# First batch of a block-sorted attention with a gated MLP: V blocks by transposes, K copied in output order

## The chip, the cores and the metric

One Trainium2 chip, one of its cores. The metric is the device time of one execution in microseconds (us), and the time of a kernel is the median of its runs. A profile is one execution taken by the hardware profiler; it names the engines PE (TensorE matmul), PEld (TensorE weight load), DVE (VectorE), ACT (ScalarE), POOL (GpSimd) and SP (the queue of SyncE, from which some DMAs are issued).

## The reference, cut to what matters

```python
B, H, S, D = 4, 8, 768, 64;  n_blocks = 8;  block = 96
P = sort_net                                   # [B, H, 8, 8]
for _ in range(5):                             # exp, then rows and columns normalised
    P = exp(P - max);  P = P / (rowsum + 1e-9);  P = P / (colsum + 1e-9)
k_sorted = einsum('bhij,bhjcd->bhicd', P, k_blocks)     # blocks of K and V are mixed by P
v_sorted = einsum('bhij,bhjcd->bhicd', P, v_blocks)
scores = q_blocks @ k_sorted^T / sqrt(D)                # within each block of 96 rows
x = softmax(scores) @ v_sorted                          # -> [B, S, H*D]
h = relu(x @ w_in);  u, v = halves of h                 # w_in [512, 1024]
v_n = layer-normalised v
v_s = w_spatial @ v_n + b_spatial                       # w_spatial [768, 768]
out = (u * v_s) @ w_out                                 # w_out [512, 512]
```

## The kernel before, in words

The four batches go through two stages. Attention of batch b makes x; the MLP (class `Gmlp`) of batch b is interleaved with the attention of batch b + 1, step by step, in an order written out by hand. Attention of batch 0 has no MLP beside it: it is a stretch of its own at the start of the kernel. PE, DVE, ACT and POOL each run their instructions in the order of the program; only the DMAs of SP are free of that order.

**Loads.** `load_heads` (L88) brings q, k or v of one batch from DRAM and casts it to bf16: 768 KB each in SBUF. All these loads are issued from POOL, one behind the other, in the order q0, v0, k0, w_in (1,024 KB), v1, w_spatial (1,152 KB), q1, k1, w_out (512 KB). The row p of such a tile holds the six sequence rows 6p to 6p+5 (index g), so a block of 96 rows takes 16 partitions.

**P.** `sinkhorn` (L149) normalises P on DVE and ACT. `spread` (L173) turns all 4 x 8 matrices with eight small matmuls, copies the result, spreads it over the partitions with one more matmul and copies it to `prep_sb`. `make_pdiag` (L191) multiplies it with a mask: `pdiag[b]` holds, for each head, a 128 x 128 matrix that mixes the eight blocks. For batch 0 this is four products on DVE of two heads each; for batches 1 to 3 it is one product of eight heads each on POOL, which are issued at the same point of the program. POOL then makes `b_bc`, a reordered copy of b_spatial.

**Attention.** Heads go in pairs (hp 0 to 3).

- `vmix` mixes V of a pair on PE (two matmuls of 384 columns) and copies the result to `vm`. After each second pair, SP writes half of `vm` to DRAM (`vd`, L245) and reads it back as `vb` (L246), with the 96 rows of a block on 96 partitions.
- `qtr` (L251) transposes q of two pairs.
- `ktr` (L266) mixes and transposes K of a pair in one go: twelve matmuls with K as the weights and `pdiag` as the data, into a PSUM tile with columns (g, it). One copy of 768 elements per partition (L277) reorders it to (it, g), the order of the sequence. The copy's loops run in the order of its source: PSUM is read in one run, and SBUF is written in steps of six elements (12 bytes).
- `score` n takes half the blocks of a pair: eight matmuls and an exp on ACT. `attend` n multiplies with `vb` on PE (eight matmuls), and DVE divides by the row sums (a reciprocal and a product).
- `xtr` transposes x of two pairs; the MLP needs all of it.

PSUM has four buffers, which all steps take in turn (`ps_tile`, L77). `warm` issues matmuls whose results nobody reads.

**The order for batch 0** (L438 to 455): sinkhorn, qtr 0 and 1, six warm matmuls, `spread`, the products of batch 0 on DVE and of the others on POOL, all four vmix, then ktr, score and attend, and xtr 0 and 1. For each later batch the steps stand in the list at L460; there `load` fetches q, k and v of batch b + 2, once the `vb` of batch b + 1 has arrived.

Of the kernel before, what the change touches and what calls it, by code (L numbers as in the profile page):

```python
# [9 lines left out]
BF16 = mybir.dt.bfloat16  # L10
# [19 lines left out]
def kernel(  # L30
# [27 lines left out]
    VW = D + 1  # L58
# [14 lines left out]
    small = ctx.enter_context(tc.tile_pool(name="small", bufs=4))  # L73
# [3 lines left out]
    def ps_tile(dt=FP32):  # L77
        return psum.tile([128, 2, 512 if dt == FP32 else 1024], dt, name="ps", tag="ps")
# [6 lines left out]
    b_nat = pers.tile([128, S], FP32)  # L85
    nc.sync.dma_start(out=b_nat, in_=_raw_ap(moe_b_spatial, 0, [[0, 128], [1, S]]))

    def load_heads(x, b, name):  # L88
        t = ld.tile([128, H, G * D], BF16, name=name, tag=name)
        nc.gpsimd.dma_start(  # L90
            out=t,
            in_=_raw_ap(x, b * H * S * D, [[G * D, 128], [S * D, H], [1, G * D]]),
        )
        return t

    v_in, k_in, q_in = {}, {}, {}

    ident_bf = const.tile([128, 128], BF16)
    make_identity(nc, ident_bf)
    a16 = const.tile([16, 128], BF16)  # L100
# [2 lines left out]
        out=a16.rearrange("p (j t) -> p j t", t=TB),  # L103
        in_=a16.rearrange("p (j t) -> p j t", t=TB),
# [3 lines left out]
    sel16 = const.tile([8, 128], BF16)  # L108
# [17 lines left out]
    q_in[0] = load_heads(q, 0, "q_in")  # L126
    v_in[0] = load_heads(v, 0, "v_in")
    k_in[0] = load_heads(k, 0, "k_in")
    w_in_sb = pers.tile([128, KC, DFF], BF16)
    nc.gpsimd.dma_start(out=w_in_sb, in_=moe_w_in.rearrange("(kc p) f -> p kc f", p=128))  # L130
    v_in[1] = load_heads(v, 1, "v_in")
    wsp_nat = pers.tile([128, G, S], BF16)
    nc.gpsimd.dma_start(out=wsp_nat, in_=moe_w_spatial.rearrange("(p g) s -> p g s", g=G))
    q_in[1] = load_heads(q, 1, "q_in")
    k_in[1] = load_heads(k, 1, "k_in")
# [35 lines left out]
    prep_sb = pers.tile([128, NB * BH], BF16)  # L171

    def spread():  # L173
        pt_ps = ps_tile()
        for i in range(NB):
            nc.tensor.matmul(
                pt_ps[0:NB, 0, i * BH:(i + 1) * BH],
                lhsT=p_bf[:, i, :], rhs=ident_bf[0:BH, 0:BH],
                start=True, stop=True,
            )  # L180
        pt_sb = pers.tile([NB, NB * BH], BF16)
        nc.vector.tensor_copy(out=pt_sb, in_=pt_ps[0:NB, 0, 0:NB * BH])
        warm(2)
        prep_ps = ps_tile()
        nc.tensor.matmul(prep_ps[:, 0, 0:NB * BH], lhsT=sel16, rhs=pt_sb, start=True, stop=True)
        nc.vector.tensor_copy(out=prep_sb, in_=prep_ps[:, 0, 0:NB * BH])
        warm(4)

    pdiag = [pd_pool.tile([128, H, NB, TB], BF16, name="pdiag") for _ in range(B)]

    def make_pdiag(b, eng, h0, n):  # L191
        eng.tensor_mul(  # L192
            out=pdiag[b][:, h0:h0 + n],
            in0=_raw_ap(mask16, 0, [mask16.ap[0], [0, n], [TB, NB], [1, TB]]),
            in1=_raw_ap(prep_sb, b * H + h0, [prep_sb.ap[0], [1, n], [BH, NB], [0, TB]]),
        )

    b_bc = pers.tile([128, S], FP32)
# [21 lines left out]
    class Attention:  # L220
        def __init__(self, b):
            self.b = b
            self.pd = pdiag[b].rearrange("p h i t -> p h (i t)")
            self.vm = vm_tiles[b % 2]
            self.q, self.k, self.e = {}, {}, {}

        def vmix(self, hp, eng):
            t = ps_tile()
# [34 lines left out]
                self.q[hp] = qT[:, x, :].rearrange("p (g i t) -> p i g t", g=G, i=NB)  # L263
            copy(eng, qT, t[:, :, 0:S])

        def ktr(self, hp, eng):  # L266
            t = ps_tile().rearrange("p x c -> p (x c)")
            for g in range(G):
                for hh in range(2):
                    nc.tensor.matmul(  # L270
                        t[hh * 64:hh * 64 + 64, g * 128:(g + 1) * 128],
                        lhsT=k_in[self.b][:, 2 * hp + hh, g * D:(g + 1) * D],
                        rhs=self.pd[:, 2 * hp + hh, :],
                        start=True, stop=True,
                    )
            kT = qk_pool.tile([128, S], BF16, name="kT", tag="k")
            copy(  # L277
                eng,
                kT.rearrange("p (it g) -> p g it", g=G),
                t[:, 0:S].rearrange("p (g it) -> p g it", g=G),  # L280
            )
            self.k[hp] = kT

        def score(self, n):
            hp, ih = n // 2, n % 2
# [150 lines left out]
    with tc.manual_schedule(engines={ET.PE, ET.DVE, ET.Activation, ET.Pool}):  # L436
        a = Attention(0)
        sinkhorn()  # L438
        warm(4)
        a.qtr(0, ACT), a.qtr(1, ACT)  # L440
        warm(6)
        spread()
        for h in range(0, H, 2):
            make_pdiag(0, DVE, h, 2)
        for b in range(1, B):
            make_pdiag(b, nc.gpsimd, 0, H)
        nc.gpsimd.tensor_copy(
            out=b_bc.rearrange("p (g c) -> p g c", g=G),
            in_=b_nat.rearrange("p (c g) -> p g c", g=G),
        )  # L450
        a.vmix(0, ACT), a.vmix(1, DVE), a.vmix(2, ACT), a.vmix(3, DVE)
        a.ktr(0, ACT), a.ktr(1, DVE), a.score(0), a.score(1), a.ktr(2, DVE), a.ktr(3, DVE)
        a.score(2), a.score(3), a.score(4), a.attend(0), a.score(5), a.attend(1)
        a.attend(2), a.score(6), a.attend(3), a.score(7), a.attend(4), a.attend(5)
        a.xtr(0, ACT), a.attend(6), a.attend(7), a.xtr(1, ACT)
        for b in range(B):
            m = Gmlp(b)
            last = b == B - 1
            a = None if last else Attention(b + 1)
            steps = """  # L460
                vproj0 vmix0 vproj1 vmix1 vmix2 vproj2 vmix3 qtr0 norm wsp0 uproj0 ktr0 ktr1 wsp1
                uproj1 qtr1 score0 score1 wsp2 uproj2 ktr2 ktr3 wsp3 load uproj3 score2 score3
                wsp4 wsp5 spatial0 attend0 attend1 score4 score5 spatial1 attend2
                attend3 spatial2 score6 score7 attend4 attend5 spatial3 attend6 attend7 xtr0
                oproj0 oproj1 xtr1 oproj2
            """.split()
            for step in steps:
                name, n = step.rstrip("0123456789"), int(step[-1]) if step[-1].isdigit() else None
                if name == "wsp":
                    if b == 0:  # L470
                        wsp_unit(n)
                elif name == "load":
                    if b + 2 < B:
                        gate = small.tile([1, 2], BF16, name="gate", tag="gate")
                        nc.gpsimd.tensor_copy(out=gate[:, 0:1], in_=a.vb[0:1, 0, 1, 0, 0:1])  # L475
                        v_in[b + 2] = load_heads(v, b + 2, "v_in")
                        q_in[b + 2] = load_heads(q, b + 2, "q_in")
                        k_in[b + 2] = load_heads(k, b + 2, "k_in")
                elif name in ("vproj", "uproj"):
                    getattr(m, name)(n)  # L480
                elif name == "spatial":
                    m.spatial(n, DVE if last and n == FC - 1 else nc.gpsimd)
                elif name == "norm":
                    m.norm()
                elif name == "oproj":
                    m.oproj(n, ACT)
                elif not last:
                    if name in ("vmix", "ktr"):
                        getattr(a, name)(n, ACT if n % 2 == 0 else DVE)
                    elif name in ("qtr", "xtr"):  # L490
                        getattr(a, name)(n, DVE)
                    else:
                        getattr(a, name)(n)
# [30 lines left out]
```

## Time and profile before

| | us |
|---|---|
| median of 3 runs | 217.22 (214.38 to 217.23) |
| profiled execution, its own time | 216.15 |
| its span, from the first to the last instruction | 214.4 |
| PE busy in the span | 167.0 (78%) |
| DVE busy | 128.6 (60%) |
| ACT busy | 94.1 (44%) |
| POOL busy | 47.7 (22%) |
| mean clock granted to TensorE | 0.884 of full speed |

Starts are counted from the first instruction. The 1.75 us between the execution's time and its span lie around the span. [...] Busy shares are averages over stretches with different limits, so the views below go by stretch.

### The profile page before, as it was taken

Reading aid. Unit: us, or ns where it says so; the run is one execution under the profiler, and the core shown is the slowest. Engines: PE = TensorE matmul, PEld = TensorE weight load, DVE = VectorE, ACT = ScalarE, POOL = GpSimd, SP = SyncE. Lnnn points to the kernel's source line nnn. Section 1 sums busy time; section 2 is a strip of 40 time slices with the busy share of each in tenths; the row PEclk is TensorE's granted clock in tenths of the full one; section 3 lists DMA queues with packets and bytes.
Section 4 is the critical chain, followed back from the end, with each engine's and each line's share of the span. In section 5 each row is a group of like instructions: output and inputs, shape, how many; then the busy total and the mean of one; then the engine's idle time right before and its main releaser. Section 6 shows DMA issues by size and latency. Waiting matters only on the chain.

```text
span 214.4 us, 3826 instructions
## 1 busy us (share of the span) xinstructions
PE 167.0 (78%) x1621; PEld 102.0 (48%) x1630; DVE 128.6 (60%) x229; ACT 94.1 (44%) x105; POOL 47.7 (22%) x46
## 2 busy tenths in 40 slices
PE   3293550189894988999986889999868898999981
PEld 0250250177353556665454566555535665556530
DVE  4719974066179856782598548717965586185430
ACT  3151570053457484105666842148649321446031
POOL 8809500000000313350000535300000363000710
PEclk9999555555599799999998799999979999999998
DMA  5999999980006399404236798052550000510015
GB/s 99 201 204 211 221 238 235 213 152 0 0 3 213 85 169 202 76 0 196 102 133 168 103 204 136 0 199 98 173 130 0 3 0 2 234 63 0 0 71 222
DMA packets 23041, 25.50 MB, mean 119 GB/s; under 512 B 753, under 2 KB 19697, under 8 KB 22897
## 3 DMA queue, kind: packets, MB, share of 16 engines
q0 software_dynamic: 13680, 12.19, 35.9%
q1 hardware_dynamic: 9344, 13.08, 18.7%
q8 instruction: 12, 0.20, 0.4%
q14 instruction: 5, 0.03, 0.1%
HBM read 27.98 MB, written 9.49 MB: 175 GB/s over the span
## 4 chain that ended last, share of the span: by engine, by line
PE 49%; DVE 22%; DMA 14%; ACT 9%; POOL 3%; issue 2%; DVEq 0%; ACTq 0%; SPq 0%; POOLq 0%
PE ps L402 13%; PE ps L355 9%; PE ps L423 8%; PE ps L387 7%; DMA vb<-vd 6%; DMA vd<-vm 4%; DVE vs L408 4%; DVE kT L215 4%; ACT kT L213 4%; DMA q_in<-in_q_dram 4%; DVE pdiag L192 3%; DVE vm L215 3%; PE ps L313 3%; POOL gt L412 2%; DVE stats L366 2%; PE ps L335 2%
## 5 line engine op out<-in xcount | busy, mean ns | idle before, releaser
L412 POOL TENSOR_TENSOR gt<-vs,u_sb 128x768 bf16<-128x768 f32 x15 | 24.6, 1640 | 79.0 <-DVE rec L321 57.0
L298 ACT ACTIVATE ex<-ps 96x768 bf16<-96x768 f32 x32 | 24.3, 804 | 33.5 <-PE ps L291 22.3
L402 PE MATMUL ps<-wspT,v_sb 128*128 128x384 bf16 x192 | 33.3, 326 | 1.7 <-ACT ex L298 1.4
L387 PE MATMUL ps<-xt,w_in_sb 128*128 128x384 bf16 x128 | 26.4, 359 | 4.9 <-DVE kT L215 2.7
L215 DVE CAST kT<-ps 128x768 bf16<-128x768 f32 x9 | 24.3, 2726 | 9.4 <-PE ps L270 9.4
L366 DVE BATCH_NORM_STATS2 stats<-v_sb 128x6 f32<-128x512 bf16 x24 | 16.2, 676 | 18.5 <-ACT v_sb L363 18.4
L213 ACT COPY o_sb<-ps 128x1024 f32<-128x1024 f32 x12 | 12.1, 1012 | 33.4 <-PE ps L423 33.4
L408 DVE TENSOR_TENSOR vs<-ps,b_bc 128x768 f32<-128x768 f32 x16 | 15.3, 958 | 18.2 <-PE ps L402 18.0
L313 PE MATMUL ps<-vb,ex 96*96 96x65 bf16 x256 | 17.1, 225 | 10.5 <-DMA vb<-vd 10.0
L355 PE MATMUL ps<-w_in_sb,xt 128*128 128x512 bf16 x92 | 24.2, 405 | 1.3 <-ACT xt L213 1.1
L402 PEld LDWEIGHTS <-v_sb 128*128 128x128 bf16 x192 | 18.3, 98 | 12.9 <-issue 1.6
L423 PE MATMUL ps<-w_out_sb,gt 128*128 128x512 bf16 x92 | 22.5, 379 | 1.9 <-POOL gt L412 1.0
L322 DVE TENSOR_TENSOR x_sb<-ps,rec 96x512 bf16<-96x512 f32 x32 | 22.0, 687 | 1.1
L313 PEld LDWEIGHTS <-ex 96*96 96x96 bf16 x256 | 16.1, 142 | 12.3 <-DMA vb<-vd 10.3
L213 ACT CAST kT<-ps 128x768 bf16<-128x768 f32 x7 | 19.1, 2728 | 2.3 <-PE ps L270 2.3
L387 PEld LDWEIGHTS <-w_in_sb 128*128 128x128 bf16 x128 | 12.8, 104 | 14.4 <-issue 8.0
L393 ACT ACTIVATE u_sb<-ps 128x768 bf16<-128x768 f32 x16 | 13.6, 873 | 9.6 <-PE ps L387 9.6
L291 PE MATMUL ps<-qT,kT 64*96 64x96 bf16 x256 | 12.1, 228 | 7.3 <-ACT kT L213 5.0
L363 ACT ACTIVATE v_sb<-ps 128x1024 bf16<-128x1024 f32 x12 | 12.3, 1023 | 10.1 <-PE ps L355 10.1
L355 PEld LDWEIGHTS <-xt 128*128 128x128 bf16 x96 | 9.8, 104 | 13.0 <-issue 2.1
L475 POOL COPY gate<-vb 1x1 bf16<-1x1 bf16 x2 | 0.4, 178 | 69.6 <-DMA vb<-vd 69.6
L423 PEld LDWEIGHTS <-gt 128*128 128x128 bf16 x96 | 8.6, 98 | 12.8 <-POOL gt L412 3.1
(66 smaller groups left out, 179.0 us busy)
## 6 DMA issues: line engine op xcount, KB each, us to landing
out_dram<-o_sb SPq DMA_DIRECT2D x12, 512.0 KB, 2.8
vd<-vm SPq DMA_DIRECT2D x8, 390.0 KB, 2.8
vb<-vd SPq DMA_DIRECT2D x8, 390.0 KB, 4.2
q_in<-in_q_dram POOLq DMA_DIRECT2D x4, 768.0 KB, 10.6
v_in<-in_v_dram POOLq DMA_DIRECT2D x4, 768.0 KB, 8.9
k_in<-in_k_dram POOLq DMA_DIRECT2D x4, 768.0 KB, 13.6
wsp_nat<-in_moe_w_spatial_dram POOLq DMA_DIRECT2D x1, 1152.0 KB, 25.9
w_in_sb<-in_moe_w_in_dram POOLq DMA_DIRECT2D x1, 1024.0 KB, 17.3
```

The costliest lines, as they stand in the source:

```text
L213: nc.scalar.copy(out=out, in_=in_)
L215: nc.vector.tensor_copy(out=out, in_=in_)
L298: nc.scalar.activation(out=e.rearrange("p h i c -> p h (i c)"), in_=t[0:BLK, :, 0:NB // 2 * BLK], func=AF.Exp, scale=scale,)
L313: nc.tensor.matmul(t[0:BLK, hh, ii * VW:(ii + 1) * VW], lhsT=self.e[n][:, hh, ii, :], rhs=self.vb[:, i, h // (H // 2), h % (H // 2), :], s ...
L322: nc.vector.tensor_mul(out=self.x[:, ih * (NB // 2):(ih + 1) * (NB // 2), hp * 128:hp * 128 + 128] .rearrange("p i (h d) -> p h i d", h=2) ...
L355: nc.tensor.matmul(t[:, x, :], lhsT=self.xt[kc][:, g * 128:(g + 1) * 128], rhs=w_in_sb[:, kc, DH:DFF], start=(kc == 0), stop=(kc == KC - 1),)
L366: nc.vector.bn_stats(out=stats, in_=v_sb[:, x, :])
L387: nc.tensor.matmul(t[:, x, 0:HW], lhsT=w_in_sb[:, kc, mc * 128:(mc + 1) * 128], rhs=self.xt[kc][:, x * HW:(x + 1) * HW], start=(kc == 0), ...
L402: nc.tensor.matmul(t[:, x, 0:HW], lhsT=self.v[g][:, mc * 128:(mc + 1) * 128], rhs=wspT[:, g, x * HW:(x + 1) * HW], start=(g == 0), stop=(g ...
L408: nc.vector.tensor_add(out=vs, in0=t[:, :, 0:HW], in1=b_bc.rearrange("p (x c) -> p x c", x=2),)
L412: eng.tensor_mul(out=gt.rearrange("p (x c) -> p x c", x=2), in0=vs, in1=self.u[mc].rearrange("p (x c) -> p x c", x=2),)
L423: nc.tensor.matmul(t[:, x, :], lhsT=self.gt[mc][:, g * 128:(g + 1) * 128], rhs=w_out_sb[:, mc, :], start=(mc == 0), stop=(mc == FC - 1),)
```

## The change

- Loads are issued in the order q0, k0 (both ahead of the constants that POOL builds), v0, w_in, w_spatial, v1, k1, q1, w_out.
- `spread(b, nb)` handles nb batches from b on. Batch 0 goes first, alone; batches 1 to 3, with their products on POOL and the copy `b_bc`, follow at the step `spread` in the middle of the attention of batch 0. The products of batch 0 on DVE are two: heads 0 and 1, and heads 2 to 7. Ten of the twelve warm matmuls around `spread` are dropped.
- `mixed_t` is the old `ktr`, now for K or V. Its copy names the loops in the order of its output: SBUF is written in one run, and PSUM is read in steps of 128 elements (512 bytes). All batches use it for K.
- In batch 0, V takes the way of K: `vtr` mixes and transposes it, and `vblk` transposes each block back (eight transposes of 128 x 96 and one copy of 96 x 1,024 into `vb`). `vmix` with its two DMAs per half is not used in batch 0; the later batches keep it.
- The attention of batch 0 has a new order, given as a string; A and D name the engine that copies.

```diff
+    q_in[0] = load_heads(q, 0, "q_in")
+    k_in[0] = load_heads(k, 0, "k_in")
     ident_bf = const.tile([128, 128], BF16)
...
+    vb0 = att.tile([BLK, NB, 2, H // 2, VW], BF16, name="vb", tag="vb")
+    nc.vector.memset(vb0[:, :, :, :, D:VW], 1.0)
...
-    def spread():
+    def spread(b, nb):
+        n = nb * NB * H
         pt_ps = ps_tile()
         for i in range(NB):
             nc.tensor.matmul(
...
-                lhsT=p_bf[:, i, :], rhs=ident_bf[0:BH, 0:BH],
+                lhsT=p_bf[:, i, :], rhs=ident_bf[0:BH, b * H:(b + nb) * H],
...
-        def ktr(self, hp, eng):
+        def mixed_t(self, src, hp, eng):
             t = ps_tile().rearrange("p x c -> p (x c)")
...
-                kT.rearrange("p (it g) -> p g it", g=G),
-                t[:, 0:S].rearrange("p (g it) -> p g it", g=G),
-            )
-            self.k[hp] = kT
+                kT.rearrange("p (it g) -> p it g", g=G),
+                t[:, 0:S].rearrange("p (g it) -> p it g", g=G),
+            )
+            return kT
+
+        def ktr(self, hp, eng):
+            self.k[hp] = self.mixed_t(k_in, hp, eng)
+
+        def vtr(self, hp, eng):
+            self.vT[hp] = self.mixed_t(v_in, hp, eng)
+
+        def vblk(self, hp, eng):
+            half, h0 = hp // 2, 2 * hp % (H // 2)
+            if hp == 0:
+                self.vb = vb0
+            t = ps_tile(BF16)
+            for i in range(NB):
+                nc.tensor.transpose(
+                    t[0:BLK, 0, i * 128:(i + 1) * 128], self.vT[hp][:, i * BLK:(i + 1) * BLK],
+                    ident_bf,
+                )
+            copy(
+                eng, self.vb[:, :, half, h0:h0 + 2, 0:D],
+                t[0:BLK, 0, :].rearrange("p (i h d) -> p i h d", i=NB, h=2),
+            )
...
-        warm(6)
-        spread()
-        for h in range(0, H, 2):
-            make_pdiag(0, DVE, h, 2)
-        for b in range(1, B):
-            make_pdiag(b, nc.gpsimd, 0, H)
...
+        spread(0, 1)
+        make_pdiag(0, DVE, 0, 2), make_pdiag(0, DVE, 2, 6)
+        warm(2)
+        order = """
+            ktr0A vtr0D ktr1A vtr1A score0 vblk0D score1 ktr2D attend0 score2 attend1 score3 vblk1D
+            vtr2A attend2 ktr3A attend3 score4 spread vblk2D score5 attend4 vtr3A attend5 score6
+            score7 vblk3D attend6 xtr0A attend7 xtr1D
+        """
...
+            if name == "spread":
+                spread(1, 3)
+                for b in range(1, B):
+                    make_pdiag(b, nc.gpsimd, 0, H)
```

## Rows read from the trace of the kernel before

**Rows 1.** The chain that ended last, first 55 us: start, us, what

```profile
1.80 7.80 DMA q_in<-in_q_dram
...
25.14 9.56 DMA vd<-vm
34.72 12.45 DMA vb<-vd
...
53.00 1.45 ACT xt L213
```

**Rows 2.** Stretches of 2 us: busy PE, PEld, DVE, ACT, POOL; clock, DMA share, GB/s

```profile
20.00:22.00 2.00, 0.79 (x2) 0.11 (x2) 2.00 (x2) 0.07 (x1) 2.00 (x2) 0.79 1.17 205
...
36.00:38.00 2.00, 0.00 (x0) 0.00 (x0) 0.00 (x0) 0.00 (x0) 0.00 (x0) 0.50 1.26 209
```

**Rows 3.** Line 192, the products: ns min/median/max, first and last start

```profile
L192 DVE TENSOR_TENSOR pdiag<-mask,prep_sb x4: 425/2222/2226, 16.3 to 21.0; 128x256 bf16<-128x256 bf16 x4
L192 POOL TENSOR_TENSOR pdiag<-mask,prep_sb x3: 2179/2184/2237, 16.4 to 20.7; 128x1024 bf16<-128x1024 bf16 x3
```

**Rows 4.** The tile k_in: its four loads on POOL, and us from issue to landing

```profile
L90 POOL DMA_DIRECT2D k_in<-in_k_dram x4: 881/898/933, 4.1 to 119.7; - x4
...
DMA to landing us min/median/max: 13.2/13.6/36.3
```

**Rows 5.** DVE's instructions, shapes apart: busy us, mean ns, idle before

```profile
L215 DVE CAST kT<-ps 128x768 bf16<-128x768 f32 x9 | 24.3, 2726 | 9.4 <-PE ps L270 9.4
L322 DVE TENSOR_TENSOR x_sb<-ps,rec 96x512 bf16<-96x512 f32 x32 | 22.0, 687 | 1.1
...
L215 DVE CAST vm<-ps 128x768 bf16<-128x768 f32 x8 | 7.5, 940 | 0.0
...
L321 DVE RECIPROCAL rec<-ps 96x8 f32<-96x8 f32 x32 | 6.3, 196 | 10.7 <-PE ps L313 10.5
...
L215 DVE COPY xt<-ps 128x1536 bf16<-128x1536 bf16 x6 | 5.7, 950 | 7.4 <-PE ps L335 7.4
...
L157 DVE TENSOR_REDUCE colsum<-p_all 32x8 f32<-32x64 f32 x5 | 1.3, 253 | 0.1
...
L152 DVE TENSOR_REDUCE rowsum<-p_all 32x8 f32<-32x64 f32 x5 | 1.0, 207 | 2.3 <-ACT p_all L151 2.3
...
L153 DVE RECIPROCAL rowsum<-rowsum 32x8 f32<-32x8 f32 x5 | 1.0, 191 | 0.2
```

**Rows 6.** ACT's instructions, shapes apart: the copy of transposed K

```profile
L213 ACT CAST kT<-ps 128x768 bf16<-128x768 f32 x7 | 19.1, 2728 | 2.3 <-PE ps L270 2.3
```

**Rows 7.** PE's timeline: start, us, line, shapes, count, idle before

```profile
28.47 1.49 PE L270 MATMUL ps<-pdiag,k_in 128*64 128x128 bf16 x24
29.89 0.88 PE L291 MATMUL ps<-qT,kT 64*96 64x96 bf16 x16
...
43.11 1.49 PE L313 MATMUL ps<-vb,ex 96*96 96x65 bf16 x16
...
51.52 1.45 PE L335 MATMUL ps<-ident_bf,x_sb 96*128 96x96 bf16 x16 [0.27 <-ACT xt L213]
...
79.95 0.87 PE L204 MATMUL ps<-ident_bf,wsp_nat 128*128 128x128 bf16 x12
```

**Rows 8.** Waits of PE from 54 to 214.4: us in total, times, longest

```profile
PE ps L291 <- ACT kT L213: 2.9, 5, 1.0
PE ps L387 <- DVE kT L215: 2.7, 2, 1.4
...
PE ps L387 <- ACT kT L213: 1.9, 1, 1.9
```

**Rows 9.** Stretches of 4 us, columns as in rows 2

```profile
54.00:58.00 4.00, 3.50 (x9) 1.35 (x10) 0.00 (x0) 1.17 (x2) 0.00 (x0) 0.50 0.00 0
...
66.00:70.00 4.00, 1.83 (x32) 1.41 (x32) 4.00 (x10) 3.35 (x2) 0.00 (x0) 0.87 0.71 199
70.00:74.00 4.00, 3.94 (x53) 2.35 (x52) 3.26 (x3) 1.19 (x2) 0.81 (x2) 0.70 0.45 100
```

More of the change, by code (lines that the diff above doesn't have):

```diff
@@ L124 @@
         vm_tiles.append(vm)
-    q_in[0] = load_heads(q, 0, "q_in")
+    vb0 = att.tile([BLK, NB, 2, H // 2, VW], BF16, name="vb", tag="vb")
+    nc.vector.memset(vb0[:, :, :, :, D:VW], 1.0)
     v_in[0] = load_heads(v, 0, "v_in")
-    k_in[0] = load_heads(k, 0, "k_in")
     w_in_sb = pers.tile([128, KC, DFF], BF16)
     nc.gpsimd.dma_start(out=w_in_sb, in_=moe_w_in.rearrange("(kc p) f -> p kc f", p=128))
-    v_in[1] = load_heads(v, 1, "v_in")
     wsp_nat = pers.tile([128, G, S], BF16)
     nc.gpsimd.dma_start(out=wsp_nat, in_=moe_w_spatial.rearrange("(p g) s -> p g s", g=G))
+    v_in[1] = load_heads(v, 1, "v_in")
+    k_in[1] = load_heads(k, 1, "k_in")
     q_in[1] = load_heads(q, 1, "q_in")
-    k_in[1] = load_heads(k, 1, "k_in")
     w_out_sb = pers.tile([128, FC, DM], BF16)
@@ L169, in warm @@
             nc.tensor.matmul(t[:, 0, :], lhsT=ident_bf, rhs=warm_sb, start=True, stop=True)
-    prep_sb = pers.tile([128, NB * BH], BF16)
-    def spread():
+    prep_sb = pers.tile([128, B, NB, H], BF16)
+    def spread(b, nb):
+        n = nb * NB * H
         pt_ps = ps_tile()
@@ L176, in spread @@
             nc.tensor.matmul(
-                pt_ps[0:NB, 0, i * BH:(i + 1) * BH],
-                lhsT=p_bf[:, i, :], rhs=ident_bf[0:BH, 0:BH],
+                pt_ps[0:NB, 0, 0:n].rearrange("p (b i h) -> p b i h", i=NB, h=H)[:, :, i, :],
+                lhsT=p_bf[:, i, :], rhs=ident_bf[0:BH, b * H:(b + nb) * H],
                 start=True, stop=True,
             )
-        pt_sb = pers.tile([NB, NB * BH], BF16)
-        nc.vector.tensor_copy(out=pt_sb, in_=pt_ps[0:NB, 0, 0:NB * BH])
-        warm(2)
+        pt_sb = small.tile([NB, B * NB * H], BF16, name="pt", tag="pt")
+        nc.vector.tensor_copy(out=pt_sb[:, 0:n], in_=pt_ps[0:NB, 0, 0:n])
         prep_ps = ps_tile()
-        nc.tensor.matmul(prep_ps[:, 0, 0:NB * BH], lhsT=sel16, rhs=pt_sb, start=True, stop=True)
-        nc.vector.tensor_copy(out=prep_sb, in_=prep_ps[:, 0, 0:NB * BH])
-        warm(4)
+        nc.tensor.matmul(prep_ps[:, 0, 0:n], lhsT=sel16, rhs=pt_sb[:, 0:n], start=True, stop=True)
+        nc.vector.tensor_copy(
+            out=prep_sb[:, b:b + nb].rearrange("p b i h -> p (b i h)"), in_=prep_ps[:, 0, 0:n],
+        )
     pdiag = [pd_pool.tile([128, H, NB, TB], BF16, name="pdiag") for _ in range(B)]
@@ L194, in make_pdiag @@
             in0=_raw_ap(mask16, 0, [mask16.ap[0], [0, n], [TB, NB], [1, TB]]),
-            in1=_raw_ap(prep_sb, b * H + h0, [prep_sb.ap[0], [1, n], [BH, NB], [0, TB]]),
+            in1=_raw_ap(prep_sb, b * NB * H + h0, [prep_sb.ap[0], [1, n], [H, NB], [0, TB]]),
         )
@@ L224, in __init__ @@
             self.vm = vm_tiles[b % 2]
-            self.q, self.k, self.e = {}, {}, {}
+            self.q, self.k, self.e, self.vT = {}, {}, {}, {}
         def vmix(self, hp, eng):
@@ L271, in ktr @@
                         t[hh * 64:hh * 64 + 64, g * 128:(g + 1) * 128],
-                        lhsT=k_in[self.b][:, 2 * hp + hh, g * D:(g + 1) * D],
+                        lhsT=src[self.b][:, 2 * hp + hh, g * D:(g + 1) * D],
                         rhs=self.pd[:, 2 * hp + hh, :],
@@ L440 @@
         a.qtr(0, ACT), a.qtr(1, ACT)
-        warm(6)
-        spread()
-        for h in range(0, H, 2):
-            make_pdiag(0, DVE, h, 2)
-        for b in range(1, B):
-            make_pdiag(b, nc.gpsimd, 0, H)
-        nc.gpsimd.tensor_copy(
-            out=b_bc.rearrange("p (g c) -> p g c", g=G),
-            in_=b_nat.rearrange("p (c g) -> p g c", g=G),
-        )
[L451 to L455, printed above, removed]
+        spread(0, 1)
[6 more added lines that the diff above has]
+        """
+        for step in order.split():
+            name, rest = step.rstrip("0123456789AD"), step.lstrip("abcdefghijklmnopqrstuvwxyz")
+            if name == "spread":
+                spread(1, 3)
+                for b in range(1, B):
+                    make_pdiag(b, nc.gpsimd, 0, H)
+                nc.gpsimd.tensor_copy(
+                    out=b_bc.rearrange("p (g c) -> p g c", g=G),
+                    in_=b_nat.rearrange("p (c g) -> p g c", g=G),
+                )
+            else:
+                getattr(a, name)(int(rest[0]), *[{"A": ACT, "D": DVE}[e] for e in rest[1:]])
         for b in range(B):
```

## The prediction

> **What bounds the kernel now.** I read the chain that ended last first, because the edit sits in one stretch. In its first 55 us it is no engine's work: V leaves through DRAM at 25.14, the write takes 9.56 us and the read back 12.45 us, and only at 54.45 (53.00 + 1.45) is x of batch 0 ready for the MLP [rows 1]. Then the stretches: from 36 to 38 no compute engine runs at all, while the DMA engines move 209 GB/s, which is the weight and batch 1 loads [rows 2]. So the round trip of V is slow because it shares the DMA engines with loads nobody needs yet, and PE stands idle behind it, at the 0.50 clock. Third, the waits of PE after 54 us: 2.9 + 2.7 + 1.9 = 7.5 us of its idle time ends with a copy of transposed K [rows 8], and that copy costs 2,726 ns on DVE and 2,728 ns on ACT for 768 elements, where the `vm` copy of the same size from PSUM takes 940 ns on DVE [rows 5, 6]. Two engines of different speed giving the same time says that an operand's path, not the engine, sets it.
>
> **The start.** The products of batch 0 leave the path. The first one took 425 ns; the other three took 2,222 ns each, the length of one POOL product (2,184 ns), with which they alternate [rows 3]. With POOL's products moved behind, I cost the two at 0.43 us and about 1.1 us (three times 0.35 of slope plus a start). If they stayed at 2.2 us per two heads, they would end near 19.4. P is ready at about 11 us as before; two PE steps and two small copies bring the products to 12.9 (heads 0, 1) and 14.2 (the rest). That is not what the attention then waits for. The loads are: q0 lands at 9.60 (1.80 + 7.80) [rows 1], and k0, two loads later, at 4.1 + 13.2 = 17.3 [rows 4], so a load of 768 KB takes 3.85 us, which agrees with 205 GB/s [rows 2]. The change issues q0 about one DMA issue earlier (0.9 us [rows 4]; the constants behind it on POOL are not needed before q0 lands), so q0 lands at 8.6, k0 at 12.4 and v0, now third, at 16.3; 17.3 if nothing is won at the front. PE is in order and `vtr0` is its second step, so PE's real start is **16.3**. An early start of the normalisation's 8 KB load could be disturbed by q0; some 3 us of cover hide that.
>
> By the same rate the other loads land at 21 (w_in), 27 (w_spatial), 31 (v1), 35 (k1) and 39 (q1), because 1.56 MB of round trips no longer share the engines. Batch 1 takes v1 first and q1 about 8 us after its MLP starts, so the new order of loads costs nothing unless the attention ends before 31.
>
> **The attention of batch 0, at the low clock.** PE's new prices, from rows at 0.50: K or V mixed, 1.49 / 2 = 0.75; a score 0.44; an attend 1.49 / 2 = 0.75; an xtr 1.4 [rows 7]. `vblk` is not in the trace; its eight transposes lie between half of an xtr (0.73) and twice 8 x 0.0725 from the twelve 128-wide transposes of w_spatial at the full clock (1.16) [rows 7]; I take 1.0. From 16.3 on PE has: V 4 x 0.75, K 3 x 0.75, scores 8 x 0.44, vblk 4 x 1.0, attends 8 x 0.75, xtr 2 x 1.4, the second spread 0.5: 22.1 us, which ends at 38.4 with no gap.
>
> The gaps come from DVE. The copy of `vblk` is not in the trace either: 0.66 us at the rate of the x copy (950 ns for 1,536 bf16 elements), 1.2 at one element per 1.04 ns plus a start, as the f32 copies have it; its rows of 64 inside 65 are not one run, so I take 1.2. An attend costs DVE 0.196 + 0.687 us less the overlap of the two, 0.81 [rows 5]. Stepping through the order string, each engine in order and PSUM's four buffers in turn, PE waits before attend2 (0.6), behind the second spread (0.6), before attend4 (0.9), attend6 (1.3) and xtr1 (0.9), each time for a `vblk` copy or the divide ahead of it, and the last copy adds 1.0. Sum: 38.4 + 4.3 + 1.0 = **43.8**. With the vblk copy at 0.66 it is 42.1. Against 54.45 that is 10.6 us earlier.
>
> Costed at nothing: POOL's products for batches 1 to 3 (3 x 2.18 us [rows 3]) and `b_bc` (from about 30, under the rest of the attention; batch 1 needs its product at about 45). DVE's work beside them reads PSUM; the `vm` copies that ran beside POOL's `b_bc` before do not stand out of their mean of 940 ns [rows 5]. If each POOL instruction did hold one DVE instruction as the products did, it would be 2 us each, four times, at most 8. The dropped warm matmuls cost clock if PE was going to keep it, which is the second case below.
>
> **The copy in output order, the disputed price.** No row shows a long read of PSUM in steps. The nearest is the reciprocal of the row sums: it reads PSUM in steps of 65 elements, and takes 196 ns for eight, against 191 for eight from SBUF in one run [rows 5]: at most 0.6 ns more per element. The column sum reads SBUF in steps and takes 253 against 207 ns for 64 elements, 0.7 ns more per element. So the new copy lies between 0.94 us (steps free) and 1.5 us, and its ends are 0.94 and, were the read as dear as the write is now, 2.73 or beyond. I take 0.95, nearest to the reciprocal. In the attention of batch 0, 1.4 in its place gives 44.0, so the slack there hides this.
>
> [...]
>
> **Batches 1 to 3.** Of the 7.5 us of PE's waits for K copies I count 6 as gone; the rest turns into waits for DVE, which is busy all 4.00 us of the stretch 66 to 70. The clock adds to it: in that stretch PE is busy 1.83 of 4.00 us and the granted clock falls to 0.87, then 0.70 [rows 9], which is (0.13 + 0.30) x 2 x 4 = 3.4 us at the low level. Batches 2 and 3 show the same dip, so about 10 us run at half speed and cost up to 5; I count 4. Together **10 us**, with ends of 3 (the waits only move) and 12.
>
> **The sum.** 216.15 - 10.6 - 10 = 195.5 us, against the profiled execution; it lies 1.1 below the median of 217.22, within the spread of the three runs. Other attention ends and batch gains put this case between 190 and 201.
>
> **The rivals.**
>
> *The clock stays high in the first attention.* Before, it fell when PE had little to do while waiting for products (busy 0.79 of 2.00, clock 0.79 [rows 2]). The new order is denser, but PE still waits from 13 to 16.3 for v0. At the full clock PE's steps roughly halve, DVE (14.8 us of work after 16.9) becomes the limit, and the same stepping ends at 36.1. Gain: 18.3, and 1.9 more because the first 3.8 us of the MLP, at 0.50 before [rows 9], run at full speed; with the 10 of the batches **186**.
>
> *The stepped read is dear too.* At 2.0 us a copy, a little over midway between 0.94 and 2.73, the attention ends at 46.3 (gain 8.2) and the batches give 3.4: 204.5. At 2.73, the copy gains nothing: the attention ends at 50.6, and 216.15 - 3.9 = **212**. For it: the old copy shows how dear a step can be; against it: the reciprocal.
>
> *The stepped read is dearer than the stepped write: slower than before.* At c us a copy, the attention ends at 50.6 + 6 x (c - 2.73), and two copies of each later batch stand on the path, 6 x (c - 2.73) more. It breaks even at c = 3.05 and passes 2% at about 3.4 (4.5 ns per element); at 4.0 it is 216.15 + 3.8 + 7.6 = **227.5**.
>
> *It does not do what it says:* the attention ends early, but batch 1 waits for its loads. If the loads kept ending at 47, q1 would land near 44; the MLP from 43.8 needs it at 52. This is out of the way unless the high clock holds too, and then costs 2.
>
> **How the numbers follow.** The forecast 195.5 has 0.50, the high clock 0.25, the dear read 0.19 (two thirds of it below 212), the dearer read 0.05, the rest 0.01. The range 184 to 206 leaves out the upper part of the dear read and the slower case. Faster by over 2% (below 212.9): 0.50 + 0.25 + 0.13 = 0.88; within: 0.07; slower: 0.05. Two per cent is about what separates a change from the spread of runs here (214.38 to 217.23).
>
> **What would show it.** The K copy at 0.8 to 1.0 us on both engines; DVE products of 0.4 and about 1.1 us with POOL idle beside them; no DMA of `vd` before batch 1; `vtr0` starting with v0's landing near 16.3; x of batch 0 copied by 44; loads done by 42; no dip of the clock at the K copies of later batches. Wrong would be: a K copy over 1.5 us, PE waiting at batch 1 for v1, k1 or q1, or a `vblk` copy far over 1.2 us.

## The result and the profile after

The changed kernel takes **189.91 us** (median; 189.3 to 191.81) against 217.13: a ratio of **0.879**, 95% interval 0.870 to 0.888. Ratios and intervals here come from the fast executions of each kernel alone, so they are not exactly the quotients of the medians. The forecast was 195.5 within 184 to 206. The profiled execution took 189.82 with a span of 188.1, so 26.3 us of span are gone.

The chain that ended last, first 45 us of the changed kernel (start, us, what), answers to [rows 1]:

```profile
4.23 14.14 DMA v_in<-in_v_dram
18.37 0.04 issue
18.41 2.13 PE ps L274 x36
...
40.25 0.97 DVE xt L219
...
41.27 2.62 PE ps L381 x6
```

V's two DMAs are gone from it. What stands at its head is the load of V; x of batch 0 is ready at 41.22 in place of 54.45. So 13.2 us come from the start, and the other 13.1 from what follows (214.4 - 54.45 = 159.95 before, 188.1 - 41.22 = 146.9 after). The forecast had 10.6 and 10.

Instructions of DVE and of ACT in the changed kernel, shapes apart (busy us, mean ns, idle before), for [rows 5, 6]:

```profile
L219 DVE CAST kT<-ps 128x768 bf16<-128x768 f32 x8 | 7.7, 956 | 8.8 <-PE ps L274 8.8
L219 DVE CAST vm<-ps 128x768 bf16<-128x768 f32 x6 | 5.6, 932 | 0.0
L219 DVE COPY vb<-ps 96x1024 bf16<-96x1024 bf16 x4 | 2.8, 689 | 3.0 <-PE ps L301 3.0
```

```profile
L217 ACT CAST kT<-ps 128x768 bf16<-128x768 f32 x12 | 9.5, 796 | 6.5 <-PE ps L274 6.5
L217 ACT CAST vm<-ps 128x768 bf16<-128x768 f32 x6 | 4.8, 805 | 0.0
```

The disputed price is settled by the first two lines: the copy that reads PSUM in steps takes 956 ns, and `vm`, which reads it in runs, 932. On ACT it is 796, against 805 for `vm`. The two engines now differ as they do for `vm`; before, both stood at 2.73 us. The `vblk` copy takes 0.69 us, close to the lower of its two bounds (0.66).

PE's waits after 41 us in the changed kernel (us in total, times, longest) answer to [rows 8]:

```profile
PE ps L274 <- DVE vm L219: 2.4, 3, 0.9
PE ps L428 <- ACT ex L324: 1.6, 4, 0.5
PE ps L413 <- DVE kT L219: 0.8, 2, 0.4
```

The 7.5 us of waits for K copies have become 0.8. And the clock, of which the page gives one digit per slice of 1/40 of the span, no longer dips after the start:

```profile
PEclk9999996558999999999999999999999999999998
```

But it falls once, in the attention of batch 0. PE's timeline there (start, us, line, shapes, count, idle before), and the stretches of 2 us with the columns of [rows 2]:

```profile
18.41 0.85 PE L274 MATMUL ps<-pdiag,v_in 128*64 128x128 bf16 x12 [2.44 <-DMA v_in<-in_v_dram]
...
23.23 0.55 PE L339 MATMUL ps<-vb,ex 96*96 96x65 bf16 x8
23.71 0.38 PE L317 MATMUL ps<-qT,kT 64*96 64x96 bf16 x8
...
25.53 0.53 PE L274 MATMUL ps<-pdiag,v_in 128*64 128x128 bf16 x12
...
28.34 0.35 PE L180 MATMUL ps<-ident_bf,p_bf 32*8 32x24 bf16 x8
29.38 0.25 PE L188 MATMUL ps<-pt,sel 8*128 8x192 bf16 x1 [0.69 <-DVE pt L186]
...
31.08 0.77 PE L339 MATMUL ps<-vb,ex 96*96 96x65 bf16 x8 [0.30 <-DVE vb L219]
31.78 0.85 PE L274 MATMUL ps<-pdiag,v_in 128*64 128x128 bf16 x12
```

```profile
26.00:28.00 2.00, 1.42 (x30) 1.23 (x28) 1.33 (x3) 1.07 (x2) 0.00 (x0) 1.00 1.00 194
28.00:30.00 2.00, 1.31 (x28) 1.02 (x25) 1.61 (x5) 1.32 (x2) 0.00 (x0) 1.00 1.26 197
30.00:32.00 2.00, 1.70 (x26) 1.49 (x26) 0.83 (x3) 0.81 (x1) 1.89 (x1) 0.50 1.32 205
```

PE waits 2.44 us for V at the head, and 0.69 us in the second spread, which stands behind a divide on DVE; right after that the clock is at 0.50, and it stays there until 43.6. Cut into stretches of half a microsecond, the rows of the clock say 1.00 or 0.50 in the traces before and after alike, and something between only where it changes; these two are called the high and the low level here. The durations say more than the rows: twelve matmuls of a pair take 0.85 us at V's landing, as they do at 31.8 where the rows show 0.50, and 0.53 at 25.5, and eight attend matmuls go from 0.55 at 23.2 to 0.77 at 31.1. So PE's matmuls take the low level's durations up to about 23, though its rows say 1.00, then the high one's, and from 30 on the low one's again. The two waits are what the second half of the experiments is about.

### The profile page after: what moved, and what is told of

It reads as the page before. It is cut to its first block, busy times and chain, and to the rows that moved or that the text cites. A ratio compares the mean times of both kernels' runs of the same rounds, so it can differ in the third digit from the quotient of the medians.

```text
span 188.1 us, 3963 instructions
## 1 busy us (share of the span) xinstructions
PE 160.3 (85%) x1692; PEld 102.1 (54%) x1701; DVE 108.8 (58%) x232; ACT 82.5 (44%) x107; POOL 46.9 (25%) x46
## 4 chain that ended last, share of the span: by engine, by line
PE 55%; DVE 24%; DMA 8%; ACT 4%; POOL 4%; issue 2%; DVEq 0%; ACTq 0%; POOLq 0%
PE ps L428 15%; PE ps L381 10%; PE ps L449 9%; DMA v_in<-in_v_dram 8%; PE ps L413 7%; DVE vs L434 5%; PE ps L339 4%; DVE stats L392 3%; DVE x_sb L348 3%; PE ps L274 3%; DVE v_sb L403 3%; DVE vm L219 3%; POOL gt L438 3%; PE ps L317 2%; ACT ex L324 2%
## 5 line engine op out<-in xcount | busy, mean ns | idle before, releaser
L381 PE MATMUL ps<-w_in_sb,xt 128*128 128x512 bf16 x92 | 23.6, 397 | 0.8 <-DVE xt L219 0.6
L413 PE MATMUL ps<-xt,w_in_sb 128*128 128x384 bf16 x128 | 23.0, 326 | 1.0 <-DVE kT L219 0.8
L339 PE MATMUL ps<-vb,ex 96*96 96x65 bf16 x256 | 16.4, 217 | 2.1 <-DVE vb L219 1.7
L339 PEld LDWEIGHTS <-ex 96*96 96x96 bf16 x256 | 15.4, 133 | 4.2 <-issue 2.1
L413 PEld LDWEIGHTS <-w_in_sb 128*128 128x128 bf16 x128 | 12.0, 97 | 8.7 <-issue 1.1
L419 ACT ACTIVATE u_sb<-ps 128x768 bf16<-128x768 f32 x16 | 12.6, 806 | 8.1 <-PE ps L413 8.1
L219 DVE CAST kT<-ps 128x768 bf16<-128x768 f32 x8 | 7.7, 956 | 8.8 <-PE ps L274 8.8
L217 ACT CAST kT<-ps 128x768 bf16<-128x768 f32 x12 | 9.5, 796 | 6.5 <-PE ps L274 6.5
L262 PE MATMUL ps<-ident_bf,q_in 128*64 128x128 bf16 x192 | 7.9, 244 | 4.8 <-DMA q_in<-in_q_dram 4.4
## 6 DMA issues: line engine op xcount, KB each, us to landing
q_in<-in_q_dram POOLq DMA_DIRECT2D x4, 768.0 KB, 10.6
v_in<-in_v_dram POOLq DMA_DIRECT2D x4, 768.0 KB, 11.1
wsp_nat<-in_moe_w_spatial_dram POOLq DMA_DIRECT2D x1, 1152.0 KB, 23.2
```

The costliest lines, as they stand in the source:

```text
L339: nc.tensor.matmul(t[0:BLK, hh, ii * VW:(ii + 1) * VW], lhsT=self.e[n][:, hh, ii, :], rhs=self.vb[:, i, h // (H // 2), h % (H // 2), :], s ...
L381: nc.tensor.matmul(t[:, x, :], lhsT=self.xt[kc][:, g * 128:(g + 1) * 128], rhs=w_in_sb[:, kc, DH:DFF], start=(kc == 0), stop=(kc == KC - 1),)
L413: nc.tensor.matmul(t[:, x, 0:HW], lhsT=w_in_sb[:, kc, mc * 128:(mc + 1) * 128], rhs=self.xt[kc][:, x * HW:(x + 1) * HW], start=(kc == 0), ...
```

## The experiments

Times are medians; ratios are to the kernel before, run on the same chip. The changed kernel, in this measure, is 189.9 and 0.879. The kernel before took 217.1, 216.6, 215.5 and 216.3 in the four sets of runs, so a difference between medians of two sets is sure to about a microsecond.

**What each part is worth.** Theory: two gains of about 13 us that have little to do with each other, the copy order in batches 1 to 3 and V's way in batch 0. Rival: the later gain follows from the quicker start.

*The copy order alone*, on the kernel before:

```diff
-                kT.rearrange("p (it g) -> p g it", g=G),
-                t[:, 0:S].rearrange("p (g it) -> p g it", g=G),
+                kT.rearrange("p (it g) -> p it g", g=G),
+                t[:, 0:S].rearrange("p (g it) -> p it g", g=G),
```

> The kernel before with one edit: the copy of transposed K in output order. Theory (the later batches are worth about 13 us by the copy alone, batch 0 hides its K copies behind V's way through DRAM): 217.1 - 13 = 204, within 202 to 206, the attention of batch 0 still ending near 54, and no dip of the clock in the later batches. Rival (the copy gives only the 7.5 us of PE waits named in the trace, the rest of the later gain comes from the new start): 208 to 210.

Measured: **204.7**, 0.9465 (0.941 to 0.952), 11.9 us below the 216.6 of the kernel before in that set. x of batch 0 is ready at 55.2, no earlier than before. The clock on the page is low in the start alone:

```profile
PEclk9999575555579999999999999999999999999999
```

So the copy is worth 12 us by itself, all of it after batch 0. It is also the size of what was read in the trace: 6.7 us of PE's waits gone (7.5 less the 0.8 that are left, in this run's trace too) and about 5 for the clock's dips, as the prediction estimated them.

*The old copy order, everywhere or in the later batches only*, on the changed kernel (the diff above reversed; in the second for `self.b > 0`):

> The changed kernel with the copy in the old order everywhere, so 8 copies of K and V in batch 0 and 12 of K later take 2.73 us again. Theory: 13 us more in the later batches and about 8 in the attention of batch 0, where four copies stand on DVE's and four on ACT's path: 189.9 + 21 = 211 (207 to 214). Rival (batch 0 has slack for them since PE waits for DVE anyhow): 202 to 204.

Measured: **208.75**, 0.963 (0.958 to 0.969): 18.8 us back. x is ready at 51.0 instead of 41.2, and after it 156.0 us pass instead of 146.9, but not the 159.95 of the kernel before. The clock on its page says where the difference may lie: it is up again less than 1.8 us into the MLP (4.2 before; the first six matmuls behind x take 2.25 us there and 2.74 before), and dips once later, not three times.

```profile
PEclk9997555555999999999996999999999999999999
```

> The changed kernel, batch 0 with the new copy, batches 1 to 3 with the old one. Theory: the 13 us of the later batches come back and nothing else: 203 (201 to 205), x of batch 0 still copied at 41.2, and the clock dips again at the K copies of each batch. Rival (part of the later gain came with the quicker start and stays): 196 to 199.

Measured: **200.1**, 0.923 (0.917 to 0.929); the profiled execution took 202.5, the other three 199.2 to 200.9. So 9 to 10 us come back, with x ready at 40.9 in the profile. This is 2 to 3 us less than the copy gave on the kernel before, below the range that the theory gave, and just above the rival's 196 to 199: most of the later gain is the copy's own, and some 2 us of it may hang on the clock at which the later batches are met; that was not tried by itself.

In the first of the two x comes 9.8 us later. Not all of it is the eight copies of batch 0: V landed 0.8 us later there (19.20), and PE was at the low level from then on (the twelve matmuls of a pair take 0.86 us at 26.05, eight attend matmuls 0.77 at 39.56). Two runs further down (the gated one and the one with the issues late) were at the low level for the whole attention too, and took 24.1 and 25.2 us from V's landing to x; this one took 31.8, so the copies cost about 7. Its x at 51.0 is no earlier than the 51.15 of the next run, which sends V by DRAM with the new copy order, and with V by DRAM the copy order did not move x (54.45 and 55.2 above). So without the new order V's way over PE would have gained next to nothing. That is an inference: no run has V by DRAM with the old copies and the rest of the change.

*V by DRAM, the rest as changed*: the order string of batch 0 is

```diff
+            vmix0A vmix1D vmix2A vmix3D ktr0A ktr1D score0 score1 ktr2D ktr3D spread score2 score3
+            score4 attend0 score5 attend1 attend2 score6 attend3 score7 attend4 attend5
+            xtr0A attend6 attend7 xtr1A
```

> The changed kernel, but V of batch 0 goes by vmix and DRAM as before, with the old order of steps; POOL's products stay late, the copy order and the order of the loads stay new. Theory (the round trip, slowed by the loads, sets the attention's end): vb of the second half lands at 44 to 47 and x is ready at 51 to 54, so 189.9 + 11 = 201 (199 to 203). Rival (the products on POOL were what made the round trip late, and with them gone it starts 4 us earlier and ends earlier): x at 45 to 47, 194 to 196.

Measured: **201.0**, 0.928 (0.923 to 0.933). The chain of that run has the same round trip as [rows 1], only earlier:

```profile
21.50 9.78 DMA vd<-vm
31.29 12.59 DMA vb<-vd
...
49.70 1.45 ACT xt L217
```

9.78 + 12.59 us against 9.56 + 12.45, with no POOL product beside it: POOL does not make it slow. The loads are what is left. On the page of the kernel before the same two transfers take 2.8 and 4.2 us in the median of all batches; the loads of batches 2 and 3 are held back until such a round trip is over. No run held back the loads of batch 0, so their part is read from this and not tested. x is ready at 51.15. V's way over PE is thus worth 201.0 - 189.9 = **11.1 us**, given the rest. The step from the copy alone to this run, 204.7 to 201.0, has the size by which the round trip starts earlier: this write begins at 21.50 and not at 25.14 as before. The products of batch 0 no longer stand at its head (DVE ends them at 15.07), but V's load does, which lands at 17.57; the new order of the loads is in that step too, and was not tried by itself.

**What the start costs.** After these, 189.9 still held two losses, V's landing and the clock.

*POOL's products early*: P is spread for all batches at first, and POOL's products start beside DVE's.

```diff
-        spread(0, 1)
+        spread(0, 4)
         make_pdiag(0, DVE, 0, 2), make_pdiag(0, DVE, 2, 6)
+        for b in range(1, B):
+            make_pdiag(b, nc.gpsimd, 0, H)
...
-                spread(1, 3)
-                for b in range(1, B):
-                    make_pdiag(b, nc.gpsimd, 0, H)
```

> The changed kernel, but all four batches of P are spread at first and POOL's products start beside DVE's, as before. Theory (since V of batch 0 lands at 18.4, the products of heads 2 to 7 may be late until 19): DVE's second product waits for one POOL product of 2.2 us, ends near 18, nobody waits for it, and the spread in the middle (0.7 us of wait on PE, 0.7 us on DVE) is saved: 188.5 to 190.5. Rival (moving POOL's products away was worth the 3.7 us by which two of the runs above differ): 193 to 194.

Measured: **184.1**, 0.853 (0.846 to 0.859), clearly below the changed kernel: undoing this part of the change gains 5.8 us. Its products (ns min/median/max, first and last start) and two of the same stretches:

```profile
L196 POOL TENSOR_TENSOR pdiag<-mask,prep_sb x3: 2007/2237/2720, 15.8 to 20.7; 128x1024 bf16<-128x1024 bf16 x3
L196 DVE TENSOR_TENSOR pdiag<-mask,prep_sb x2: 424/1592/2761, 15.8 to 16.1; 128x256 bf16<-128x256 bf16 x1, 128x768 bf16<-128x768 bf16 x1
```

```profile
28.00:30.00 2.00, 1.53 (x33) 1.34 (x31) 1.86 (x4) 1.92 (x3) 0.00 (x0) 1.00 1.23 196
30.00:32.00 2.00, 2.00 (x47) 1.77 (x47) 1.43 (x4) 1.39 (x3) 0.00 (x0) 1.00 1.32 205
```

DVE's second product does wait for POOL, 2.76 us in place of 0.95, and nobody needs it before V lands. The spread in the middle is gone, the clock stays at 1.00, and x is ready at 37.1. The theory had the sign and missed the size: it had priced the wait, not the clock.

*Warm matmuls in PE's waits* of batch 0 (two behind `ktr0`, two each ahead of attend2, attend4, attend6 and xtr1, three in the second spread):

```diff
+        if b:
+            warm(3)
         prep_ps = ps_tile()
...
-            ktr0A vtr0D ktr1A vtr1A score0 vblk0D score1 ktr2D attend0 score2 attend1 score3 vblk1D
-            vtr2A attend2 ktr3A attend3 score4 spread vblk2D score5 attend4 vtr3A attend5 score6
-            score7 vblk3D attend6 xtr0A attend7 xtr1D
+            ktr0A warm vtr0D ktr1A vtr1A score0 vblk0D score1 ktr2D attend0 score2 attend1 score3 vblk1D
+            vtr2A warm attend2 ktr3A attend3 score4 spread vblk2D score5 warm attend4 vtr3A attend5 score6
+            score7 vblk3D warm attend6 xtr0A attend7 warm xtr1D
```

> The changed kernel with warm matmuls where PE waits in batch 0: two behind ktr0, two each ahead of attend2, attend4, attend6 and xtr1, three in the second spread. Theory (the fall of the clock at 30 costs the rest of this attention and the first two microseconds of the MLP): if it stays at 1.00, x is ready 3 to 4 us earlier, 185 to 187. Rival (the added matmuls stand in PE's order and take PSUM buffers, and the clock falls in any case): 190 to 192.

Measured: **185.8**, 0.861 (0.857 to 0.865). Matmuls that compute nothing make the kernel 4.1 us faster. The stretch in which the changed kernel lost the clock:

```profile
28.00:30.00 2.00, 2.00 (x30) 1.23 (x31) 1.62 (x5) 1.59 (x2) 0.00 (x0) 1.00 1.25 198
30.00:32.00 2.00, 1.84 (x35) 1.52 (x37) 1.18 (x3) 0.81 (x1) 1.56 (x1) 1.00 1.31 205
```

The second spread and POOL's late products are still in this kernel, so the clock alone is worth about 4 of the 5.8, and the place of the spread and of POOL's products the rest. The fall goes with the spread and not with a moment: in the profiles of the later-batches run above and of the K-first and bias-last runs below, which all keep the second spread in the middle, the matmuls pass from the high level's durations to the low level's right behind it, at 28.9, 26.0 and 27.1.

*The spread once, POOL's products late*: as with the early products, but a one-element copy on POOL waits for `vb` of the second pair, so that the products run from 28 on.

```diff
+                gate = small.tile([1, 2], BF16, name="gate", tag="gate")
+                nc.gpsimd.tensor_copy(out=gate[:, 0:1], in_=vb0[0:1, 0, 0, 2, 0:1])
+                for b in range(1, B):
+                    make_pdiag(b, nc.gpsimd, 0, H)
```

> As the run with POOL's products early, all of P spread at first, but POOL's products wait, by a one-element copy on POOL, for vb of the second pair, so that they run from about 26 as late as in the changed kernel. Theory (the second spread in the middle, PE standing behind DVE there, lost the clock and the time; the place of POOL's products is worth nothing): clock 1.00, 183.5 to 185.5, like the early products. Rival (late POOL products slow DVE and with it PE): 188 to 190.

Measured: 185.45 once, and 190.8 to 192.0 three times. The first is what the theory gave. The others can't be understood without the clock: in some executions of one kernel PE doesn't come up to the high level after V has landed, and the whole attention of batch 0 runs at the low one. The profiled one (191.99) is of that kind, by its matmuls; its rows of the clock say 1.00 throughout that attention (PE's timeline; its stretch from 26 to 28):

```profile
23.72 0.85 PE L339 MATMUL ps<-vb,ex 96*96 96x65 bf16 x8
24.50 0.55 PE L317 MATMUL ps<-qT,kT 64*96 64x96 bf16 x8
```

```profile
26.00:28.00 2.00, 2.00 (x28) 1.64 (x24) 1.39 (x3) 0.81 (x1) 0.00 (x0) 1.00 1.00 196
```

Eight attend matmuls take 0.85 us where the changed kernel has 0.55 at that time, and a score 0.55 where it has 0.38, and this lasts from V's landing at 18.9 into the MLP. Of the other two no trace was kept; their times put them with it. The changed kernel itself has one such execution, by its time and its mean clock: 191.81 with 0.924, where its other three have 0.96. What decides it in one execution or another, no run shows. Whether the place of POOL's products has a small price of its own stays open as well: only one execution kept the clock.

*One step moved*: `spread` stands right behind `ktr0`, where PE waits for V anyhow.

```diff
-            ktr0A vtr0D ktr1A vtr1A score0 vblk0D score1 ktr2D attend0 score2 attend1 score3 vblk1D
-            vtr2A attend2 ktr3A attend3 score4 spread vblk2D score5 attend4 vtr3A attend5 score6
+            ktr0A spread vtr0D ktr1A vtr1A score0 vblk0D score1 ktr2D attend0 score2 attend1 score3 vblk1D
+            vtr2A attend2 ktr3A attend3 score4 vblk2D score5 attend4 vtr3A attend5 score6
```

> The changed kernel with one step moved: the second spread right behind ktr0, where PE waits for V's load, in place of behind score4. Theory (same as above): the clock stays at 1.00, x ready near 36.5 to 37, 183 to 185. Rival (the clock falls because the warm matmuls are gone, wherever the spread stands): falls near 30 again, 188 to 190.

Measured: 183.5 and 183.8 with a mean granted clock of 0.99, 190.5 and 190.9 with 0.92. Where the clock is up, the theory's figure is met, in the profile (183.53) with x ready at 36.1 and matmuls at the high level's durations from 22 on; but this order doesn't make sure of it.

*K first*: three ktr and three scores ahead of the first vtr, so PE has work while V lands.

```diff
-            ktr0A vtr0D ktr1A vtr1A score0 vblk0D score1 ktr2D attend0 score2 attend1 score3 vblk1D
-            vtr2A attend2 ktr3A attend3 score4 spread vblk2D score5 attend4 vtr3A attend5 score6
+            ktr0A ktr1D score0 score1 ktr2A score2 vtr0D vtr1A score3 vblk0D vblk1D attend0 attend1
+            vtr2A attend2 ktr3A attend3 score4 spread vblk2D score5 attend4 vtr3A attend5 score6
```

> The changed kernel with another order in batch 0: three ktr and three score steps ahead of the first vtr, so that PE doesn't stand behind V's load from 16 to 18.4. Theory (the wait for V is on the path): about 2 us of PE's work move ahead, 187.5 to 188.5. Rival (DVE's copies and divides set the end of this attention, and they start with V as before): 189.4 to 190.4.

Measured: **186.2**, 0.864 (0.859 to 0.869), 3.7 us faster, more than the 2 us of work moved. x is ready at 38.0. PE has the high level's durations from 18 on and not from 23, and the clock still falls at the second spread, now at 25.

*The bias load last*: the 384 KB of the bias go to the end of POOL's queue.

```diff
-    nc.sync.dma_start(out=b_nat, in_=_raw_ap(moe_b_spatial, 0, [[0, 128], [1, S]]))
...
+    nc.gpsimd.dma_start(out=b_nat, in_=_raw_ap(moe_b_spatial, 0, [[0, 128], [1, S]]))
```

> The changed kernel with the 384 KB load of the bias moved from the start of SP's queue to the end of POOL's. Theory (V's landing is set by the bytes ahead of it at 205 GB/s): V lands 1.9 us earlier, at 16.5, and the time falls by about as much: 188.0 (187.3 to 188.7). Rival (in the first 8 us the loads are slow for another reason, the rate there is 121 to 162 GB/s): V at 18, 189.5 to 190.2.

Measured: **187.7**, 0.871 (0.865 to 0.878), 2.2 us lower by the medians and 1.6 by the ratios; the intervals overlap, so the times alone don't prove it. The mechanism shows in the trace: PE starts on q0 at 8.65 instead of 10.68 and on V at 16.32 instead of 18.41, and x is ready 2.1 us earlier, at 39.1.

```profile
8.65 2.77 PE L262 MATMUL ps<-ident_bf,q_in 128*64 128x128 bf16 x48 [2.36 <-DMA q_in<-in_q_dram]
...
16.32 0.85 PE L274 MATMUL ps<-pdiag,v_in 128*64 128x128 bf16 x12 [2.24 <-DMA v_in<-in_v_dram]
```

*The issues late*: q0 and k0 are issued behind POOL's constants, as before.

```diff
-    q_in[0] = load_heads(q, 0, "q_in")
-    k_in[0] = load_heads(k, 0, "k_in")
     ident_bf = const.tile([128, 128], BF16)
...
+    q_in[0] = load_heads(q, 0, "q_in")
+    k_in[0] = load_heads(k, 0, "k_in")
     v_in[0] = load_heads(v, 0, "v_in")
```

> The changed kernel with the issues of q0 and k0 behind POOL's constants as before, order q0, k0, v0 kept. Theory of the prediction (an earlier issue brings q0 and so V 0.9 us forward): 0.5 to 1 us slower, 190.4 to 191. Rival (the issue moved from 1.80 to 1.25 only, and q0 landed no earlier): 189.5 to 190.3, no difference that can be measured.

Measured: 189.8, 0.885 (0.875 to 0.895): no difference from the changed kernel. In its profile PE starts on q0 at 9.99 and on V at 17.65, both earlier than the 10.68 and 18.41 of the changed kernel. This profile shows in the rows of the clock, too, what the gated run showed in durations alone: a whole attention at the low level. Here PE had come up before (the twelve matmuls of `ktr0` take 0.53 us at 14.38), and the clock is lost while PE waits 2.74 us for V.

```profile
14.00:16.00 2.00, 0.58 (x13) 0.39 (x12) 1.10 (x2) 1.10 (x2) 0.00 (x0) 1.00 1.32 205
16.00:18.00 2.00, 0.35 (x8) 0.35 (x10) 0.00 (x0) 0.00 (x0) 0.00 (x0) 0.51 1.21 212
```

That execution took 192.18, and another 190.8 with the same mean clock of 0.92; the other two of this kernel took 188.4 and 188.8, with a mean clock of 0.96.

*Three edits together*: the spread behind `ktr0`, the bias last, and K first.

> Three edits of the runs together on the changed kernel: the second spread behind ktr0, the bias load last, three ktr and three scores of batch 0 ahead of the first vtr. If their gains (5.8, 2.2 and 3.7 us alone, where the last held part of the same loss of clock) add up but for the clock: 184 - 2 - 2 = 180 (178.5 to 181.5), clock 1.00. Rival (batch 1 now waits for its loads, v1 and q1): 182 to 184, with PE waiting on v_in or q_in after 32.

Measured: **180.7**, 0.844 (0.839 to 0.849), six executions within 180.3 to 181.1, the mean granted clock 0.989 or more in each. x is ready at 31.6, and from `ktr0` on no matmul of this attention takes the low level's duration. The rival is a little right as well: batch 1 now waits for q1, which lands at 39.

```profile
39.12 0.86 PE L262 MATMUL ps<-ident_bf,q_in 128*64 128x128 bf16 x24 [1.28 <-DMA q_in<-in_q_dram]
```

## Why the prediction was right, point by point

**The bound and the sign.** Right. The round trip of V was the start's bound, and it was worth 11.1 us. That the loads made it slow fits all traces, and POOL is excluded, but no run tested it. The total was short: 189.91 lies 5.6 us below the forecast's 195.5 and 3.9 above the first rival's 186.

**The start.** The products took 0.42 and 0.95 us, for the 0.43 and 1.1 that were costed; from these two a further pair of heads costs 0.26 us, where the 0.35 was the author's estimate. V's landing was wrong: 16.3 forecast, 18.41 measured. The early issue moved from 1.80 to 1.25, not by 0.9 us, and won nothing: PE started on q0 at 10.68, later than the 9.64 before. Issuing it late again changed nothing. From q0 to V it took the 7.7 us that were costed, so the whole error lies in q0's landing. The row used for it, 9.60, stands at the low end of what the runs show: with the bias ahead of q0, PE starts on it between 9.64 and 11.47 in the profiles here, whichever way it is issued, and at 8.65 and 8.67 in the two runs that load the bias last. The bytes of the bias were in that row unseen, and they, not the issue, were the thing to move.

**The attention.** 43.8 forecast (its terms add up to 43.7), 41.22 measured. That these are so close is in part luck, since two errors stand against each other: V 2.1 us late, and 22.8 us from there on where 27.5 were costed. The `vblk` copy took 0.69 and not 1.2 (four times 0.5 us); the 1.2 was at the 1.04 ns an element of the f32 copies before, which take 272 ns for 128 elements and 940 for 768. And PE's matmuls took the high level's durations from 23 to 30. The forecast and the first rival thus each hold for a part, and the time lies between their 195.5 and 186. With the clock held by warm matmuls it is 185.8, near the rival's figure, but not by the rival's sum: x is ready at 38.5 there and not at 36.1, and the batches give more than its 10. Nor are PE's steps halved at the high level, as the rival estimated: in the changed kernel a `vblk` takes 0.61 us for 1.09, a mixed pair 0.53 for 0.85, a score 0.38 for 0.55.

**Costed at nothing, or at 0.5 us: the second spread and POOL's late products.** This step failed. It named no price for the clock where PE stands behind DVE, and the stretch cost 5.8 us. The change would have been better without this part. With V where it landed, at 18.41, products left beside POOL's, which the prediction has end "near 19.4", would have delayed nobody: in the run with the early products DVE's second one ends at 18.9, before PE needs it. By the forecast's own 16.3 for V, PE would have needed them sooner; the missed landing hid that the cure was not needed. The dropped warm matmuls are a part that stays open: before, twelve of them stood around the spread, and four at 15.77 took 1.04 us, against 1.89 for four at the low level in the changed kernel (at 4.41); no run puts the ten back.

**The copy in output order.** Right: 0.96 and 0.80 us, the free end. The reciprocal's eight elements were enough to price it. For these copies the reading in steps costs 956 against 932 ns on DVE and nothing on ACT (796 against 805).

**Batches 1 to 3.** Right in kind, the term was short: 10 forecast, 11.9 measured by the copy alone. Both parts were taken with a discount, 6 of 7.5 us and 4 of 5, and hardly anything of either stayed. The time at the low level that the 4 rests on is in the trace before: the clock reads 0.50 for 3.4 us in each of three dips (from 69.0, 116.8 and 157.7). Eight matmuls with w_in take 2.72 us in the first of them, at 69.59, and 1.46 after it, at 74.48: 1.86 times as long at the low level. The 13.1 us of the two traces hold about one more, because the MLP's start runs fewer microseconds at the low clock: 2.4, where the trace before has 4.2 (54.5 to 58.7; the prediction read 3.8).

## What to carry to other kernels

Let a copy that permutes write in runs and read PSUM in steps: the order of its loops alone took it from 2.73 us to 0.96 and 0.80 and was worth 12 us here. When a wait is moved to a new place, ask what PE does there and what its clock then costs, not only how long the wait is: 0.69 us behind DVE went with a loss of clock worth about 4 us. A step with a round trip through DVE belongs where PE waits for something else anyhow: with the spread behind `ktr0` two executions of four took 183.5 and 183.8 us, the other two 190.5 and 190.9. Cure a contention only if someone waits for its victim: the product that POOL delayed took 2.76 us in place of 0.95 and was done at 18.9, before PE started on V at 19.06.

## What the runs showed of the hardware

A copy that writes 2-byte elements in steps of 12 bytes to SBUF takes 2.73 us for 768 elements on DVE and on ACT alike, 3.55 ns each; with the steps on the PSUM side it is 0.96 and 0.80. A DVE copy of 96 x 1,024 bf16 elements from PSUM into rows of 64 that start at odd multiples of 2 bytes in every second row takes 689 ns; the copies of the same type in one run take 552 ns for 768 elements and 952 for 1,536, and 689 lies on the line between them, so no price of the odd starts shows. Whether PE's clock is up in the first attention differs between executions of one kernel (183.5 us with a mean granted clock of 0.99, 190.9 with 0.92). And the rows of the granted clock can show 1.00 while matmuls take the low level's durations: in the gated run for the whole attention, in the changed kernel up to 23, where the 48 transposes of q take 2.77 us and 24 of them take 0.86 in batch 1.
